# Pooled attention with a squared-ReLU feed-forward: batch 1's values pooled on GpSimd, fillers between the stages of chunk 0's softmax, split operands of chunk 0 from block 6

## The chip, the cores and the metric

The kernel runs on one core of a Trainium2 chip. The metric is device time in microseconds (us). The three timed runs of the kernel before gave 975.21, 979.04 and 979.16 us, median 979.04. The profile shows one more execution, of 978.61 us, whose span from the first to the last instruction is 976.9 us. All durations below are from that one execution.

The engines are named as in the profile: PE is TensorE's matmul, PEld its weight load, DVE is VectorE, ACT ScalarE, POOL GpSimd, SP SyncE, which issues all DMAs here.

## The reference

Attention over keys and values pooled in groups of 8, then a feed-forward with a squared ReLU:

```python
k_p = k.reshape(B, H, Sp, pool, D).mean(axis=3)      # B=8, H=8, S=576, D=64, pool=8, Sp=72
v_p = v.reshape(B, H, Sp, pool, D).mean(axis=3)
scores = scale * np.matmul(q, k_p.transpose(0, 1, 3, 2))
scores = scores - np.max(scores, axis=-1, keepdims=True)
attn = np.exp(scores)
attn = attn / (np.sum(attn, axis=-1, keepdims=True) + 1e-09)
return np.matmul(attn, v_p).astype(np.float32)
...
x = np.ascontiguousarray(attn_out.transpose(0, 2, 1, 3)).reshape(B * S, H * D)   # 4608 x 512
h = np.maximum(x @ w_in, 0.0)                         # w_in 512 x 2048, float64 in memory
return (h * h @ w_out).astype(np.float32)             # w_out 2048 x 512, float64 in memory
```

## The kernel before, in words

The 4608 tokens are worked off in 12 chunks of 384 (`CH`). For each chunk, 16 blocks of 128 hidden columns are computed: `hidden(c, fc)` makes block fc of the hidden layer of chunk c, and `project(c, fc)` adds it to the three output tiles `o_0` to `o_2`, two steps later (`LAG`). These 192 steps are the main loop. It is written out by hand: the dictionary `work` says at which step each piece of attention for later chunks, each load and each conversion of a weight is issued, and every engine takes its instructions strictly in the order of the program (`InOrder`).

Matmuls are done in two ways. In chunk 0, blocks below `SPLIT`, a product of plain float32 operands is used: `x` with `wf`, four matmuls a block, each of which the profile shows as two passes. Everywhere else both operands are split in a high and a low part (`xh`, `xl`, `w_i`) and three products are added, twelve one-pass matmuls a block. The weights arrive as float64 and become float32 in two steps: `magnitude` (two ACT instructions for each half block, called a key here) and `to_float32` (three DVE instructions for each key). `split_weights` makes the two parts (one ACT, one DVE instruction).

Before the loop stands a prologue. It pools the keys of batch 0 on DVE (`pool_k`) and those of batch 1 on POOL (`by_halves`: add the halves of the eight rows until one is left), pools the values of batch 0 by matmuls with a matrix of ones (`pool_v_pair`, tiles `vv` to `vps`), and computes the attention of chunk 0 head pair by head pair, four pairs (`NPAIR`): `transpose_q` (`qps`), `token_scores` (`sps`), the softmax on DVE and ACT (`te`, `tm`), `token_normalise` (DVE), `token_turn` (transposes `pps`, copied to `sc` by ACT), `weigh_values` (`av`, copied to `x` by ACT). The last loop of the prologue goes over the pairs p. In it stands, before the change, `pool_v_pair(1, p)` for pairs 0 and 1 of batch 1; pairs 2 and 3 are pooled at steps 2 and 3 of the main loop. For p = 2 the magnitudes of the first two keys of weights are issued on ACT, ahead of that pair's copies of `sc`.

`keep_busy(n)` issues n matmuls of the identity with itself (tile `idle`), whose result nobody reads. Before the change it is called with 16 at the start and with 2 ahead of the first scores. Its PSUM tile is from the pool `ps_h`, which the hidden blocks use too (two buffers); `ps_a` has three buffers, for everything of the attention.

All DMAs are issued by SP in one order, each after the one eight places earlier has landed. In the prologue this order is: keys, queries and values of batch 0, keys of batch 1, the first four keys of weights, the values of batch 1 (four DMAs of two heads each), then more weights. Weights, loads and several intermediate tiles share one pool of 33 buffers (`w_tile`), so a later load can wait for the reader of an earlier tile.

Of the kernel before, what the change touches and what calls it, by code (L numbers as in the profile page):

```python
# [37 lines left out]
def pooled_attn_relu2_ffn(  # L38
# [21 lines left out]
    P = 128  # L60
# [13 lines left out]
    SCALE = 1.0 / (D ** 0.5) / POOL  # L74
    LAG, QL = 2, 4

    IDLE = (16, 2)
    STB, SCB, LD, OB = 1, 2, 4, 3


    FIRST, EAGER, AHEAD = 2, 10, 4
    PRO, RATE, MARGIN = 5, 2, 1

    SPLIT = 8


    STEADY = ((-22, -18, -14, -10), (0, 1, 3, 4, 5, 6, 7, 8))
# [95 lines left out]
    def keep_busy(n):  # L183

        for i in range(0, n):
            if i % 8 == 0:
                t = ps_h.tile([P, 512], F32, name=f"idle_{n}_{i}", tag="h")
            PE.matmul(t[:, :P], lhsT=ident, rhs=ident, start=True, stop=True)


# [15 lines left out]
    def by_halves(dst, src):  # L206

        n = POOL * D // 2
        while n > D:
            GP.tensor_tensor(src[:, :n], src[:, :n], src[:, n:2 * n], op=ALU.add)  # L210
            n //= 2
        GP.tensor_tensor(dst, src[:, :D], src[:, D:2 * D], op=ALU.add)

    def pool_k(b, i):
        if i % KT == 0:
            loaded["kp", b, i // KT] = sb.tile([QT, KT, 2, D], F32, name=f"kp_{b}_{i}", tag="kp", bufs=2)
        kp, kt = loaded["kp", b, i // KT][:, i % KT], loaded.pop(("k", b, i))
        if b == 1:
            by_halves(kp[:, 0, :], kt)
            GP.tensor_tensor(kp[:, 1, :], kt[:, :D], kt[:, D:2 * D], op=ALU.add)  # L220
        else:
            DVE.tensor_reduce(kp[:, 0, :], kt.rearrange("p (o d) -> p d o", d=D), axis=AX.X, op=ALU.add)
            DVE.tensor_copy(kp[:, 1, :], kp[:, 0, :])
# [31 lines left out]
        split(kh[:, o], kl[:, o], kf[b][:, hf, :KR])  # L255

    def pool_v(b, h):
        DVE.tensor_reduce(kv[b][2][:, h, :], loaded.pop(("v", b, h)).rearrange("p (o d) -> p d o", d=D), axis=AX.X, op=ALU.add)

# [6 lines left out]
    def load_v_pair(b, p):  # L268
        vt = loaded["v", b, p] = w_tile(F32, f"vv_{b}_{p}").rearrange("s a n -> s (a n)")[:QT, :2 * EK * D].rearrange(
            "s (h j d) -> s h j d", h=2, j=EK)  # L270
        load(vt.rearrange("s h j d -> s h (j d)"), v[b, 2 * p:2 * p + 2].rearrange("h (s j) d -> s h (j d)", j=EK))

    def pool_v_pair(b, p):
        new_batch(b)
        vt = loaded.pop(("v", b, p))
        pt = ps_a.tile([P, 512], F32, name=f"vps_{b}_{p}", tag="a")
        for j in range(EK):
            PE.matmul(pt[:SP_, :2 * D], lhsT=ones[:, j, :], rhs=vt[:, :, j, :], start=j == 0, stop=j == EK - 1)

        def then():  # L280
            ACT.copy(kv[b][2][:, 2 * p:2 * p + 2, :].rearrange("s h d -> s (h d)"), pt[:SP_, :2 * D])

        return then
# [120 lines left out]
    def token_scores(c, p):  # L404
        st = live.pop((c, p))
        ss = token_banks(c, p, "sps", "o")
        segs = segments(c)
        for t in range(NQ):
            h, b = 2 * p + t // 2, segs[t % 2 % len(segs)][0]
            for j in range(2):  # L410
                two = slice(j * D, (j + 1) * D)
                PE.matmul(ss[j][:QT, t * SP_:(t + 1) * SP_], lhsT=st[two, t * QT:(t + 1) * QT],
                          rhs=kf[b][two, h // KH, h % KH * SP_:(h % KH + 1) * SP_], start=True, stop=True)
        views = [x[:QT, :NQ * SP_].rearrange("p (t n) -> p t n", t=NQ) for x in ss]

        def then():
            m = sb.tile([QT, 4, 2, NQ], F32, name=f"tm_{c}_{p}", tag="tm", bufs=2)
            e = w_tile(F32, f"te_{c}_{p}")[:QT, :, :NQ * SP_].rearrange("p i (t n) -> p i t n", t=NQ)
            e = [e[:, i] for i in range(2)]
            for i in range(2):  # L420
                DVE.tensor_reduce(m[:, 0, i], views[i], axis=AX.X, op=ALU.max)
                if c:
                    DVE.tensor_scalar(m[:, 1, i], m[:, 0, i], -SCALE, None, op0=ALU.mult)
                else:
                    DVE.tensor_tensor(e[i], views[i], m[:, 0, i].unsqueeze(2).to_broadcast([QT, NQ, SP_]), op=ALU.subtract)
            for i in range(2):
                if c == 0:
                    ACT.activation(e[i], e[i], AF.Exp, scale=SCALE)
                for t in range(NQ if c else 0):
                    ACT.activation(e[i][:, t], views[i][:, t], AF.Exp, bias=m[:, 1, i, t:t + 1], scale=SCALE)  # L430
            live[c, p] = (e, m)

        return then
# [34 lines left out]
    def weigh_values(c, p):  # L468

        if p == 0 and c == 0:  # L470
            x0.extend(w_tile(F32, f"x_{c}_{i}")[:, :, :CH] for i in range(2))
        elif p == 0:
            xts[c] = (sb.tile([P, NPAIR, CH], F32R, name=f"xh_{c}", tag="xh", bufs=2),
                      sb.tile([P, NPAIR, CH], F32R, name=f"xl_{c}", tag="xl", bufs=2))
        sc, rb = live.pop((c, p))
        av = ps_a.tile([P, 512], F32, name=f"av_{c}_{p}", tag="a")
        for b, o, n in segments(c):
            for i in range(2):
                PE.matmul(av[i * D:(i + 1) * D, o:o + n], lhsT=kv[b][2][:, 2 * p + i, :], rhs=sc[:, i, o:o + n],
                                 start=True, stop=True)  # L480

        def then():
            if c == 0:
                ACT.copy(x0[p // 2][:, p % 2, :], av[:, :CH])
                return
            xh, xl = xts[c]
            if c == 1:
                split(xh[:, p, :], xl[:, p, :], av[:, :CH])
                return
            DVE.tensor_tensor(rb, av[:, :CH], rb, op=ALU.mult)  # L490
            split(xh[:, p, :], xl[:, p, :], rb)

        return then
# [66 lines left out]
    def at(step, f, *a):  # L560
        work.setdefault(max(step, -PRO), []).append((f, a))
# [20 lines left out]
    first_keys = keys[:FIRST]  # L582
    for key in keys[:FIRST + 2]:
        land(key)
    for p in range(NPAIR):
        load_v_pair(1, p)
    for key in keys[FIRST + 2:EAGER]:
        land(key)
    issue_loads()
# [18 lines left out]
        f()  # L608
    for i in range(NKT):
        pool_k(1, i)  # L610
    for p in range(NPAIR):
        token_normalise(0, p)
        after = [token_scores(0, p + 2), pool_v_pair(1, p)] if p + 2 < NPAIR else []
        if p:
            weigh_values(0, p - 1)()
        if p == 2:
            for key in first_keys:
                magnitude(key)
        token_turn(0, p)()
        for f in after:  # L620
            f()
    to_float32(*first_keys)
    weigh_values(0, NPAIR - 1)()
    for hf in range(2):
        at(0, transpose_k, 1, hf)
        at(9 + hf, split_k, 1, hf)
    for p in range(2, NPAIR):
        at(p, pool_v_pair, 1, p)
    at(3, split_x0)


# [42 lines left out]


    last = (to_float32, split_weights)
    on_pe = (transpose_k, transpose_q, scores, token_scores, token_turn, weigh_values, pool_v_pair)
    for s in range(-PRO, len(steps) + LAG):
        todo = work.get(s, [])
        activate = hidden(*steps[s]) if 0 <= s < len(steps) else None  # L680
# [49 lines left out]
```

## Time and profile before

| what | value |
|---|---|
| median of three timed runs | 979.04 us |
| the profiled execution, its own time | 978.61 us |
| its span | 976.9 us |
| PE busy | 957.1 us (98%) |
| DVE, ACT, POOL busy | 611.6, 451.9, 332.9 us |
| start of the first hidden block (`h`) | 51.23 us |
| mean granted TensorE clock over the span | 0.983 |

A busy share says only that instructions were under way. The views used below are the page (sums over the whole span, and the span in 40 slices), the chain of waits (followed back from the last instruction, so that each piece is what the next one waited for), the timeline of one engine (start, duration, engine, line, operation, out<-in, shapes, count, and in brackets the idle time ahead and what ended it), and the table of windows (busy time of each engine in a stretch, with the granted clock as a share of full speed). All compute instructions have line 34, that of the helper which keeps them in order, so they are told apart by their tiles.

### The profile page before, as it was taken

The page shows a single profiled execution, that of the slowest core. Times are in us where ns is not written, and L with a number is a line of the kernel's source. Part 1 is how long each engine was busy: PE and PEld are TensorE (multiplying, and loading weights), DVE is VectorE, ACT ScalarE, POOL GpSimd, SP SyncE. Part 2 cuts the span into 40 slices and gives each one's busy share as a digit, 9 for nine tenths or more (in the row PEclk, how much of TensorE's full clock was granted, in tenths as well). Part 3 has the DMA queues.
Part 4 walks back from the last instruction along what each step waited for, and adds up shares of the span by engine and source line. Part 5 has one row for each costly group of instructions (what it writes and reads, how often), then busy time and mean ns, then how long its engine had stood idle before and what let it go on. Part 6 is the DMA issues. An engine that isn't in the chain of part 4 may idle for free.

```text
span 976.9 us, 13532 instructions
## 1 busy us (share of the span) xinstructions
PE 957.1 (98%) x4980; PEld 811.7 (83%) x4980; DVE 611.6 (63%) x1028; ACT 451.9 (46%) x913; POOL 332.9 (34%) x191
## 2 busy tenths in 40 slices
PE   7799999999999999999999999999999999999998
PEld 6555667888888888888888888888888888888997
DVE  7477887667765655767775656666776555453221
ACT  2487876665344344444434444443543434432322
POOL 4100044354353453434345344433434434440000
PEclk9589999999999999999999999999999999999999
DMA  9944201112112112112212101211311210100000
GB/s 275 347 143 128 80 17 65 48 52 84 48 45 74 30 33 82 33 51 79 60 43 70 44 18 55 65 40 46 100 52 29 77 31 18 58 10 9 32 1 33
DMA packets 51810, 63.64 MB, mean 65 GB/s; under 512 B 13904, under 2 KB 32928, under 8 KB 51744
## 3 DMA queue, kind: packets, MB, share of 16 engines
q1 hardware_dynamic: 51744, 62.78, 20.8%
q8 instruction: 39, 0.64, 0.3%
q14 instruction: 27, 0.22, 0.1%
HBM read 53.08 MB, written 9.68 MB: 64 GB/s over the span
## 4 chain that ended last, share of the span: by engine, by line
PE 92%; DVE 2%; DMA 2%; ACT 2%; issue 1%; SPq 1%; ACTq 0%
PE o L34 41%; PE h L34 40%; PE av L34 4%; PE sps L34 3%; PE qps L34 1%; DMA vv<-in_v_dram 1%; PE vps L34 1%; DMA k<-in_k_dram 1%; DVE wf_o L34 1%; DVE wf_i L34 1%; DMA q<-in_q_dram 1%; PE pps L34 1%; SPq L34 1%; ACT raw_i L34 0%; DVE tm L34 0%
## 5 line engine op out<-in xcount | busy, mean ns | idle before, releaser
L34 PE MATMUL h<-xh,w_i 128*128 128x384 f32 x1472 | 411.8, 340 | 0.0
L34 PE MATMUL o<-w_o,gh 128*128 128x512 f32 x1056 | 334.8, 398 | 0.0
L34 PEld LDWEIGHTS h<-xh,w_i 128*128 128x128 f32 x1472 | 269.8, 188 | 10.1 <-issue 1.0
L34 POOL PARTITION_ALL_REDUCE tot<-sc x80 | 201.4, 2564 | 209.9 <-issue 199.5
L34 PE MATMUL h<-xl,w_i 128*128 128x384 f32 x736 | 247.2, 336 | 0.0
L34 PEld LDWEIGHTS o<-w_o,gh 128*128 128x128 f32 x1056 | 192.5, 189 | 51.9 <-issue 16.5
L34 POOL PARTITION_ALL_REDUCE mx<-sc x80 | 118.4, 1527 | 319.0 <-ACT sc L34 319.0
L34 DVE TENSOR_TENSOR gl<-r,gh 128x384 fp32r<-128x384 f32 x176 | 143.6, 816 | 109.0 <-ACT gh L34 108.7
L34 PE MATMUL o<-w_o,gl 128*128 128x512 f32 x528 | 209.1, 396 | 0.0
L34 DVE TENSOR_TENSOR r<-r 128x384 f32<-128x384 f32 x160 | 105.7, 660 | 109.0 <-ACT r L34 108.6
L34 ACT CAST gh<-r 128x384 fp32r<-128x384 f32 x176 | 90.4, 514 | 149.9 <-DVE r L34 149.4
L34 PEld LDWEIGHTS h<-xl,w_i 128*128 128x128 f32 x736 | 138.2, 188 | 10.1 <-issue 2.6
L34 ACT ACTIVATE r<-h 128x384 f32<-128x384 f32 x192 | 94.0, 489 | 100.8 <-PE h L34 99.4
L34 PEld LDWEIGHTS o<-w_o,gl 128*128 128x128 f32 x528 | 99.1, 188 | 22.2
L34 DVE TENSOR_TENSOR st<-qps,st 64x384 fp32r<-64x384 f32 x80 | 60.8, 760 | 58.2 <-ACT st L34 57.4
L34 ACT CAST st<-qps 64x384 fp32r<-64x384 f32 x80 | 59.5, 743 | 56.2 <-PE qps L34 55.7
L34 ACT CAST xh<-rb 128x384 fp32r<-128x384 f32 x40 | 20.5, 513 | 94.7 <-DVE rb L34 94.7
L34 ACT ACTIVATE sc<-sc 72x384 f32<-72x384 f32 x80 | 39.7, 525 | 46.4 <-DVE sc L34 46.4
L34 DVE TENSOR_REDUCE vp<-v 72x64 f32<-72x512 f32 x48 | 50.9, 1060 | 0.0
L34 PE MATMUL av<-sc,vp 72*64 72x384 f32 (+1 forms) x256 | 46.4, 448 | 4.0 <-ACT sc L34 2.7
L34 PE MATMUL o<-wf_o,r 128*128 128x512 f32 x96 | 44.4, 598 | 0.0
L34 DVE TENSOR_REDUCE kp<-k 96x64 f32<-96x512 f32 x42 | 43.8, 1044 | 0.3 <-DMA k<-in_k_dram 0.3
(80 smaller groups left out, 707.1 us busy)
## 6 DMA issues: line engine op xcount, KB each, us to landing
k<-in_k_dram SPq DMA_DIRECT2D x48, 192.0 KB
out_dram<-ob SPq DMA_DIRECT2D x36, 256.0 KB
raw_i<-in_moe_w_in_dram SPq DMA_DIRECT2D x16, 512.0 KB
raw_o<-in_moe_w_out_dram SPq DMA_DIRECT2D x16, 512.0 KB
rb<-rd SPq DMA_DIRECT2D x80, 96.0 KB
v<-in_v_dram SPq DMA_DIRECT2D x48, 144.0 KB
q<-in_q_dram SPq DMA_DIRECT2D x30, 192.0 KB
q<-in_q_dram SPq DMA_DIRECT2D x32, 96.0 KB
```

The lines of the kernel that those rows point to most:

```text
L34: return lambda *a, **k: self.tc.keep_in_program_order(f(*a, **k))
```

## The change

Three parts. First, batch 1's values are no longer pooled by matmuls: eight loads of one head each take the place of four of two heads, and POOL adds them up by halves, right behind batch 1's keys. Second, `keep_busy` starts with 10 matmuls where 16 were, takes its PSUM tile from `ps_a`, and is called with 2 in each of the four passes of the last prologue loop. Third, chunk 0 uses split operands from block 6 on, where it was block 8.

```diff
-    IDLE = (16, 2)
+    IDLE = (10, 2)
...
-    SPLIT = 8
+    SPLIT = 6
...
-                t = ps_h.tile([P, 512], F32, name=f"idle_{n}_{i}", tag="h")
+                t = ps_a.tile([P, 512], F32, name=f"idle_{n}_{i}", tag="a")
...
     def pool_v(b, h):
-        DVE.tensor_reduce(kv[b][2][:, h, :], loaded.pop(("v", b, h)).rearrange("p (o d) -> p d o", d=D), axis=AX.X, op=ALU.add)
+        vp, vt = kv[b][2][:, h, :], loaded.pop(("v", b, h))
+        if b == 1:
+            by_halves(vp, vt)
+        else:
+            DVE.tensor_reduce(vp, vt.rearrange("p (o d) -> p d o", d=D), axis=AX.X, op=ALU.add)
...
-    for p in range(NPAIR):
-        load_v_pair(1, p)
+    for h in range(H):
+        load_v(1, h)
...
     for i in range(NKT):
         pool_k(1, i)
+    new_batch(1)
+    for h in range(H):
+        pool_v(1, h)
     for p in range(NPAIR):
         token_normalise(0, p)
-        after = [token_scores(0, p + 2), pool_v_pair(1, p)] if p + 2 < NPAIR else []
+        after = [token_scores(0, p + 2)] if p + 2 < NPAIR else []
         if p:
             weigh_values(0, p - 1)()
+        keep_busy(IDLE[1])
         if p == 2:
...
-    for p in range(2, NPAIR):
-        at(p, pool_v_pair, 1, p)
```

What PE finds between the scores of pair 2 and the first hidden block, before the change (rows of its program: operation, out<-in, shape of the output, count; the numbers at the end of a name are buffer numbers):

```order
L34 MATMUL vps_0_342<-vv_0_110,ones 72x128 x6
L34 MATMUL pps_0_0_349<-ident,te_0_226 72x96 x4
L34 MATMUL pps_0_1_350<-ident,te_0_226 72x96 x4
```

```order
L34 MATMUL vps_1_387<-vv_1_111,ones 72x128 x6
L34 MATMUL av_0_396<-sc_0_359,vp_186 64x384 x2
L34 MATMUL pps_1_0_400<-ident,te_1_259 72x96 x4
L34 MATMUL pps_1_1_401<-ident,te_1_259 72x96 x4
L34 MATMUL av_1_428<-sc_1_410,vp_186 64x384 x2
L34 MATMUL pps_2_0_437<-ident,te_2_363 72x96 x4
L34 MATMUL pps_2_1_438<-ident,te_2_363 72x96 x4
L34 MATMUL av_2_456<-sc_2_447,vp_186 64x384 x2
```

Between the two pieces stand the scores of pair 3, unchanged. The same stretch of PE's program after the change:

```order
L34 MATMUL idle_0_364<-ident 128x128 x2
L34 MATMUL pps_0_0_367<-ident,te_0_224 72x96 x4
L34 MATMUL pps_0_1_368<-ident,te_0_224 72x96 x4
```

```order
L34 MATMUL av_0_406<-sc_0_377,vp_184 64x384 x2
L34 MATMUL idle_0_410<-ident 128x128 x2
L34 MATMUL pps_1_0_413<-ident,te_1_257 72x96 x4
L34 MATMUL pps_1_1_414<-ident,te_1_257 72x96 x4
L34 MATMUL av_1_440<-sc_1_423,vp_184 64x384 x2
L34 MATMUL idle_0_444<-ident 128x128 x2
L34 MATMUL pps_2_0_452<-ident,te_2_381 72x96 x4
L34 MATMUL pps_2_1_453<-ident,te_2_381 72x96 x4
L34 MATMUL av_2_471<-sc_2_462,vp_184 64x384 x2
```

The two groups `vps` of batch 1 are gone from PE's way, and a pair of `idle` matmuls stands ahead of each `pps`.

The second place is POOL's program behind the last key of batch 1. Before, the reductions of the main loop follow there. After the change there are 24 additions first, three for each head; these are the first six and the first of the next pair:

```order
L34 TENSOR_TENSOR v_0_110<-v_0_110 72x256
L34 TENSOR_TENSOR v_0_110<-v_0_110 72x128
L34 TENSOR_TENSOR vp_323<-v_0_110 72x64
L34 TENSOR_TENSOR v_0_110<-v_0_110 72x256
L34 TENSOR_TENSOR v_0_110<-v_0_110 72x128
L34 TENSOR_TENSOR vp_323<-v_0_110 72x64
L34 TENSOR_TENSOR v_2_111<-v_2_111 72x256
```

The third place is ACT's program at step 3 of the main loop, ahead of the read of hidden block 3 (`r_3`), after the change:

```order
L34 ACTIVATE wf_i_0_693<-raw_i_0_561 128x512
L34 ACTIVATE raw_i_0_561<-raw_i_0_561 128x512
L34 CAST w_i_0_704<-wf_i_0_604 128x512
L34 ACTIVATE r_3_709<-h_3_658 128x384
L34 ACTIVATE r_3_709<-r_3_709 128x384
```

The row `CAST w_i_0_704` is new at this place; a second one, `CAST w_i_2_766`, stands ahead of `r_4`. Each has its subtraction on DVE. Before, both casts and both subtractions came in a later step, past the end of chunk 0.

More of the change, by code (lines that the diff above doesn't have):

```diff
@@ L676, in pooled_attn_relu2_ffn @@
     last = (to_float32, split_weights)
-    on_pe = (transpose_k, transpose_q, scores, token_scores, token_turn, weigh_values, pool_v_pair)
+    on_pe = (transpose_k, transpose_q, scores, token_scores, token_turn, weigh_values)
     for s in range(-PRO, len(steps) + LAG):
```

## The prediction

> **What bounds the kernel now.** First the page: the chain of waits by engine, and the clock by slices.
>
> ```profile
> PE 92%; DVE 2%; DMA 2%; ACT 2%; issue 1%; SPq 1%; ACTq 0%
> PEclk9589999999999999999999999999999999999999
> ```
>
> PE is the bound nearly everywhere, at full clock, except in the second and third slices (24 to 73 us), where the clock was halved for a while. So I read the start closely. The table of windows, cut where the clock changed (stretch, length, then busy time with count for PE, PEld, DVE, ACT, POOL, then granted clock, DMA share, GB/s):
>
> ```profile
> 1.90:5.32 3.42, 1.94 (x9) 1.94 (x10) 3.00 (x9) 0.16 (x1) 0.00 (x0) 1.00 0.89 265
> 5.32:8.73 3.41, 3.41 (x18) 3.41 (x18) 3.31 (x7) 0.00 (x0) 0.34 (x1) 1.00 1.08 270
> 15.56:18.97 3.41, 2.37 (x26) 2.06 (x23) 2.98 (x8) 1.20 (x4) 3.01 (x7) 1.00 1.09 281
> 22.38:25.80 3.42, 0.00 (x0) 0.00 (x0) 3.25 (x10) 0.00 (x0) 3.11 (x9) 1.00 1.08 310
> 25.80:29.21 3.41, 1.40 (x7) 1.43 (x8) 0.34 (x1) 0.00 (x0) 1.96 (x5) 0.50 1.09 266
> 29.21:32.62 3.41, 3.41 (x25) 3.11 (x25) 0.00 (x0) 1.33 (x3) 0.00 (x0) 0.50 1.05 355
> 32.62:36.04 3.42, 3.42 (x22) 3.01 (x20) 2.52 (x7) 0.91 (x4) 0.00 (x0) 0.50 1.04 391
> 53.10:56.52 3.42, 3.42 (x7) 1.58 (x6) 3.38 (x7) 3.42 (x7) 0.00 (x0) 0.50 0.00 0
> 56.52:59.93 3.41, 3.41 (x19) 2.19 (x17) 3.41 (x8) 3.41 (x8) 0.00 (x0) 1.00 0.52 151
> 971.28:974.69 3.41, 1.36 (x6) 0.76 (x5) 0.00 (x0) 1.76 (x3) 0.00 (x0) 1.00 0.56 216
> 974.69:976.90 2.21, 0.00 (x0) 0.00 (x0) 0.00 (x0) 0.00 (x0) 0.00 (x0) 0.50 0.06 23
> ```
>
> The clock changed at 25.80, 56.52 and 974.69 us; the distances, 30.72 and 918.17, are 9 and 269 times 3.413 us, so it is decided window by window on a fixed grid. A window without any matmul lost it (22.38 to 25.80); so did one that was 40% busy (971.28); one 69% busy kept it (15.56). A window full of 128x128 matmuls gave it back (53.10), but windows full of the smaller `vps`, `sps`, `pps` did not (29.21, 32.62). The first recorded change is 8.73; before it the column has nothing to show, and only durations tell:
>
> ```profile
> 3.38:8.73 5.35, 5.35 (x25) 5.35 (x26) 1.00 1.02 266
> 8.73:9.60 0.87, 0.87 (x9) 0.84 (x8) 1.00 1.13 270
> ```
>
> These are the `idle` matmuls alone: 0.214 us a pass up to 8.73, 0.10 behind it. Now PE's own timeline in the prologue, and what ACT does there:
>
> ```profile
> 21.23 0.90 PE L34 MATMUL sps<-kf,st 64*96 64x72 f32 x16
> 27.81 2.81 PE L34 MATMUL vps<-vv,ones 96*72 96x128 f32 x12 [5.67 <-DMA vv<-in_v_dram]
> 30.41 1.49 PE L34 MATMUL pps<-ident,te 96*72 96x96 f32 x8
> 31.29 1.52 ACT L34 COPY sc<-pps 72x384 f32<-72x384 f32 x2 [9.15 <-PE pps L34]
> 38.45 1.51 ACT L34 COPY sc<-pps 72x384 f32<-72x384 f32 x2 [0.27 <-PE pps L34]
> 25.19 0.95 DVE L34 TENSOR_TENSOR te<-te,tm 96x288 f32<-96x288 f32 x2
> 39.34 2.22 PE L34 MATMUL av<-sc,vp 72*64 72x384 f32 x4 [0.28 <-ACT sc L34]
> 41.97 0.67 ACT L34 ACTIVATE wf_i<-raw_i 128x512 f32<-128x512 f32 x1
> 44.19 1.54 ACT L34 COPY sc<-pps 72x384 f32<-72x384 f32 x2
> 51.34 0.48 ACT L34 COPY x<-av 128x384 f32<-128x384 f32 x1 [1.63 <-PE av L34]
> 60.60 0.46 ACT L34 ACTIVATE r<-h 128x384 f32<-128x384 f32 x1
> 61.12 1.24 PE L34 MATMUL h<-x,wf_i 128*128 128x384 f32 x3 [0.17 <-ACT r L34]
> 71.59 0.82 PE L34 MATMUL pps<-ident,te 96*72 96x96 f32 x8
> 43.02 3.40 SPq L34 DMA_DIRECT2D raw_o<-in_moe_w_out_dram  x2
> ```
>
> PE stood 5.67 us for batch 1's first values, lost the clock in that wait, and everything up to 56.5 us ran at half speed. From the last copy of `x` (51.34) to the read of block 0 (60.60) ACT works without a break through seven keys' magnitudes and three copies, 9.26 us, and PE's third hidden block waits for it (61.12).
>
> **Part 1: the values leave PE.** The wait of 5.67 us and the first `vps` go, the second (2.8 us at half clock) too. What is late next is the chain `pps`, copies of `sc`, `av`, next `pps`. I walk it from the end of the scores, 22.13, less 0.4 (below). At full clock a pair of `idle` takes 0.45 (four passes of about 0.11), half a `pps` 0.5 until ACT may start (the eight take 0.82 at 71.59), the copies 1.52. At half clock ACT starts 0.9 behind `pps` (31.29 after 30.41), and `av` ends 1.6 behind its copies (39.34 + 2.22 against 38.45 + 1.51); at full clock I take 0.8.
>
> Pair 0: scores to 21.7, idle to 22.2, copies 22.7 to 24.2, `av` to 25.0, idle to 25.5. Pair 1's normalised `te` ends at 26.14 less 0.4, about then; its copies run from 26.0 to 27.5, `av` to 28.3. For pair 2 ACT first copies `x` and does the two first keys, 0.4 + 2.2 us (41.97 to 44.19), so its copies of `sc` run from 31.0 to 32.5. In the 3.4 us behind 28.7 PE has one `pps` and the start of an `av`, about 1.2 us or 35%. By the 40% row I take it that the clock falls here, near 32.5. Then `av` runs to 34.1, idle (0.85 now) to 35.0, the copies of pair 3 from 35.9 to 37.4, `av` to 39.0. The last copy of `x` then starts at 39.0 where it was 51.34: **12.3 us** earlier. ACT's 9.26 us follow unchanged, whatever PE does beside them; the first hidden block at half clock lies beside them as it did. With the clock kept all through, the same walk ends its copies at 32.5, `av` at 33.3, idle at 33.8, copies at 35.8, `av` at 36.6: 14.7 us.
>
> In the loop the other two groups go:
>
> ```profile
> 63.97 1.31 PE vps L34 x12
> 70.44 1.31 PE vps L34 x12
> 87.48 2.58 PE h L34 x8
> 131.09 2.09 PE h L34 x12
> ```
>
> They are on the chain, between blocks that PE works off back to back: **2.6 us**. What must follow faster is ACT and DVE, with these waits between 61 and 128 us:
>
> ```profile
> ACT vp L34 <- PE vps L34: 1.7, 1, 1.7
> DVE xl L34 <- ACT xh L34: 7.2, 3, 3.8
> DVE tm L34 <- PE sps L34: 1.9, 1, 1.9
> ```
>
> ACT gets 1.7 us from the very wait that goes, DVE has 3.8 in one piece: enough.
>
> POOL's additions cost by the rows of the keys:
>
> ```profile
> L34 POOL TENSOR_TENSOR k<-k 96x256 f32<-96x256 f32 x6 | 4.8, 792 | 6.0 <-DMA k<-in_k_dram 6.0
> L34 POOL TENSOR_TENSOR kp<-k 96x64 f32<-96x64 f32 x12 | 4.1, 358 | 0.5
> L34 POOL TENSOR_TENSOR k<-k 96x128 f32<-96x128 f32 x6 | 2.7, 450 | 0.5
> 36.40 0.82 DVE L34 TENSOR_TENSOR te<-te,tm 96x288 f32<-96x288 f32 x2
> ```
>
> One head is 0.79 + 0.45 + 0.36, eight heads 12.8 us, from 28 to 41 or so. The first reader is chunk 1's `av` in step 4, well behind the third hidden block, and POOL has nothing else until then (0.00 in the windows from 29.21 on): free. DVE slows a little beside POOL: the same operation took 0.95 us with POOL busy (25.19) and 0.82 without (36.40). Pair 2's `pps` may come 1.3 us late, since ACT is at the keys until 31.0, so I cost this at nothing, between 0 and 1 us. The eight loads carry the bytes of the four, the DMA engines are full either way (share above 1.0), and the weights wait behind the same bytes. One later load now waits for POOL's last addition, to 41 or 43 us, with all of SP's queue behind it; but that queue stood at 43.02 for its buffers before, and ACT takes the keys in it behind block 0.
>
> **Part 2: fillers.** Four times two `idle` are in the walk. Six fewer at the start let PE's first transposes begin at 3.38 + 20 x 0.214 = 7.65, not 9.60. The gain is between 0 and 1.95 us; DVE's pooling of the keys and the landing of batch 0's values are unmoved behind them, so I take 0.4.
>
> **Part 3: split operands.** Blocks 6 and 7 become 12 passes of 2.09 us, from 8 of 2.58: 1.0 us. Two casts and two subtractions move ahead of them, on a DVE that has at least 1.9 us of room at that place (its wait for `sps`). Between 0 and 1.0 us of gain, or 0.5 of loss if DVE becomes late; I take **0.5**.
>
> **Sum.** 12.3 + 2.6 + 0.5 = 15.4 us off the profiled execution's 978.61: **963.2 us**. That execution lies 0.4 below the median, 979.04; I leave this out.
>
> **The rivals.** *The clock holds to the end.* 14.7 + 2.6 + 0.5: 960.8 us. For it: the longest gap in the walk is under 2 us. The Trainium skill, "TensorE: Matmul & The Clock Gate", in "Why this matters for your kernels", asks only for no idle gap above some 3 us; by that rule this rival would be the forecast. Against it stands the window at 971.28, whose matmuls ended 2.05 us before the clock went.
>
> *The fillers don't do their work, and PE is never warm.* 20 cold passes are 4.27 us. One full window on the grid lies inside that only if an edge falls in the right 0.86 of 3.41 us; a window 57% busy (1.90) did not lift the clock, a full one did. If a share between is needed and is missed, the small matmuls cannot lift it later (29.21, 32.62). Then the four `vps` of batch 0 take 1.4 us more each (2.8 against 1.3 to 1.4) and the three `sps` some 0.7: the scores of pair 2 end at 22.13 + 5.6 + 2.1 = 29.8 less the 0.4 or so, and the first `pps` starts near 30.1 (30.41 before). A stage lasts 0.9 + 1.52 + 1.6 + 0.85 = 4.9, pair 2 has the keys' 2.6 ahead of its copies: `av` of pair 1 ends at 39.0, the copies at 43.1, `av` at 44.7, idle at 45.6, copies at 48.0, `av` at 49.6. The last copy of `x` starts 1.7 us earlier than before. With 3.1: 973.8 us. I hold it for the less likely case, since transposes and two more `idle` follow the burst with hardly a gap. The Trainium skill, "TensorE: Matmul & The Clock Gate", in "What's actually happening", says that at least one busy window of about 3.4 us lifts the clock and that the windows run free of the kernel's start; taken strictly, this 973.8 us would come in three executions of four, and the trace of one execution can't exclude it.
>
> *Slower: the clock is lost into the loop.* If PE, waiting for ACT behind block 1, leaves each window under the share that lifts the clock, steps 0 to 7, some 36 us of dense work from 61.12 on, run at half speed: 36 - 15 = 21 us more, 1000 us. It decides from the point where windows of `h` and `o` stay under some 60%. Against: a slowed PE fills its windows by itself, and 53.10 lifted at once.
>
> **How the numbers follow.** Forecast (clock up at the start, lost once late) 0.45; held throughout 0.25; never up 0.23; slower 0.04; the rest something unseen. The two first are 2.4 us apart; with 2 us for the bounds of parts 2 and 3 they fill 958.5 to 967. To leave out no more than 0.2 the range must reach the cold case: 958.5 to 975. A measurement can tell about 0.5%, 4.9 us, from no change, so faster means under 974.1. That holds for both first cases and about half of the cold one: 0.82; same 0.13; slower 0.05.
>
> **What would show it.** No wait of PE for `vv`; the first `h` near 39, the third near 49; granted clock 1.0 from about 9 us, perhaps 0.5 between 32 and 45; eight passes of `h` fewer ahead of step 6. Wrong would be: passes of 0.2 us behind the first burst (cold), ACT's stretch behind the last copy of `x` longer than 9.3 us, or PE waiting for `w_i` or `r` in steps 3 to 8.

## The result, and the profile after

| | before | after |
|---|---|---|
| median of the timed runs | 978.86 us (975.21 to 979.16) | 963.93 us (963.50 to 964.38) |
| ratio | | 0.9856, 95% interval 0.9832 to 0.988 |
| the profiled execution, its own time | 978.61 us | 964.33 us |
| its span | 976.9 us | 962.6 us |
| end of the last matmul | 972.64 us | 959.14 us |
| start of hidden blocks 0, 2, 3, 4, 10 | 51.23, 61.12, 67.69, 75.18, 110.42 | 39.83, 49.73, 56.20, 62.48, 96.77 |

The change takes 14.9 us off by the medians and 14.25 by the spans of the two profiled executions; 15.4 was forecast. (One execution of one experiment below, the first combination, took 3295 us, with every matmul some 2.7 times as long; its trace is left out, and no ratio counts it.)

The page of the kernel after: the chain by engine, and the granted clock by slices.

```profile
PE 88%; DVE 5%; DMA 4%; ACT 2%; issue 1%; SPq 0%; ACTq 0%; DVEq 0%
PEclk9799999999999999999999999999999999999999
```

Only the second slice (24 to 48 us) is still low, and DVE now has 5% of the chain, where it had 2. The windows, on this execution's grid (its first change of clock is at 8.99):

```profile
22.65:26.06 3.41, 3.41 (x34) 2.23 (x32) 3.27 (x9) 2.61 (x5) 3.10 (x8) 1.00 0.98 360
26.06:29.47 3.41, 2.81 (x16) 1.36 (x15) 3.21 (x8) 2.43 (x5) 2.77 (x6) 1.00 0.80 216
29.47:32.89 3.42, 1.54 (x12) 0.90 (x11) 3.25 (x10) 3.42 (x7) 3.13 (x6) 1.00 1.01 292
39.71:43.13 3.42, 3.42 (x6) 1.85 (x6) 2.00 (x3) 3.20 (x7) 3.11 (x7) 0.50 1.05 387
43.13:46.54 3.41, 3.41 (x19) 2.33 (x18) 3.41 (x5) 3.41 (x9) 3.18 (x5) 1.00 1.07 300
```

The clock goes at 32.89, behind a window in which PE was busy 1.54 of 3.42 us, and comes back at 43.13, behind a window full of `h`: 10.24 us cold, where it was 30.72. PE's own timeline, from the scores of pair 2 to the fourth hidden block, and ACT's last copy of `x` and first read of a block:

```profile
21.13 0.90 PE L34 MATMUL sps<-kf,st 64*96 64x72 f32 x16
21.96 0.71 PE L34 MATMUL idle<-ident 128*128 128x128 f32 x4
22.51 0.83 PE L34 MATMUL pps<-ident,te 96*72 96x96 f32 x8
27.54 1.57 PE L34 MATMUL av<-sc,vp 72*64 72x384 f32 x4 [0.60 <-ACT sc L34]
32.65 2.24 PE L34 MATMUL av<-sc,vp 72*64 72x384 f32 x4 [1.11 <-ACT sc L34]
34.82 1.23 PE L34 MATMUL idle<-ident 128*128 128x128 f32 x4
35.83 1.49 PE L34 MATMUL pps<-ident,te 96*72 96x96 f32 x8
39.83 4.47 PE L34 MATMUL h<-x,wf_i 128*128 128x384 f32 x8
49.73 2.85 PE L34 MATMUL h<-x,wf_i 128*128 128x384 f32 x8 [1.17 <-ACT r L34]
56.20 2.85 PE L34 MATMUL h<-x,wf_i 128*128 128x384 f32 x8 [1.04 <-ACT r L34]
39.93 0.48 ACT L34 COPY x<-av 128x384 f32<-128x384 f32 x1 [1.63 <-PE av L34]
49.18 0.51 ACT L34 ACTIVATE r<-h 128x384 f32<-128x384 f32 x1
```

The wait of 5.67 us for `vv` is gone. ACT's stretch behind the last copy of `x` is 49.18 - 39.93 = 9.25 us, the 9.26 of before. PE's wait for `r` ahead of block 2 grew from 0.17 to 1.17 us, and the one ahead of block 3 (1.04) is new. Where the time came from, by the lead over the kernel before at the same block: 11.4 us at block 0, 11.4 at block 2, 11.5 at block 3, 12.7 at block 4, 13.65 at block 10, 13.5 at the last matmul, and 0.75 more behind it. So the prologue gave 11.4, the two groups that left the loop 1.3 together, the split operands 0.8 (0.95 up to block 10; PE's wait for `te` in step 10 then grew from 1.29 to 1.56). The 0.75 is not a matter of the last stores: SP issues the last of them 0.65 us behind the last matmul and has waited for it by 2.7 us behind it, both before and after. It lies in the closing of the program, and it goes with the first part of the change: from the last matmul to the end of the span it is 3.47 to 3.49 us in all nine traces kept here with the values on POOL, 4.22 to 4.24 in all four with them on PE. Why stays open.

### The profile page after: what moved, and what is told of

Same layout as the page of the kernel before. It is cut to its first block, busy times and chain, and to the rows that moved or that the text cites. A ratio compares the mean times of both kernels' runs of the same rounds, so it can differ in the third digit from the quotient of the medians.

```text
span 962.6 us, 13481 instructions
## 1 busy us (share of the span) xinstructions
PE 946.1 (98%) x4944; PEld 803.6 (83%) x4944; DVE 615.0 (64%) x1028; ACT 451.5 (47%) x909; POOL 348.8 (36%) x215
## 4 chain that ended last, share of the span: by engine, by line
PE 88%; DVE 5%; DMA 4%; ACT 2%; issue 1%; SPq 0%; ACTq 0%; DVEq 0%
PE o L34 41%; PE h L34 39%; PE av L34 3%; PE sps L34 3%; DVE wf_o L34 2%; DVE wf_i L34 1%; PE qps L34 1%; DMA raw_o<-in_moe_w_out_dram 1%; DMA v<-in_v_dram 1%; DMA k<-in_k_dram 1%; ACT te L34 1%; DMA vv<-in_v_dram 1%; DMA raw_i<-in_moe_w_in_dram 1%; DVE tm L34 1%; DVE w_i L34 1%
## 5 line engine op out<-in xcount | busy, mean ns | idle before, releaser
L34 PE MATMUL h<-xh,w_i 128*128 128x384 f32 x1488 | 416.9, 341 | 0.0
L34 PEld LDWEIGHTS h<-xh,w_i 128*128 128x128 f32 x1488 | 272.8, 188 | 10.6 <-issue 1.4
L34 PE MATMUL h<-xl,w_i 128*128 128x384 f32 x744 | 249.9, 336 | 0.0
```

The source lines that it names most:

```text
L34: return lambda *a, **k: self.tc.keep_in_program_order(f(*a, **k))
```

## The experiments

In the table, the start of a hidden block and the end of the last matmul are read from each run's timeline, the loss of the clock from its windows; the time is the median of its own runs. The names are explained below.

| run | time, us | clock lost at (us), for | block 0 | block 3 | block 4 | block 10 | last matmul ends |
|---|---|---|---|---|---|---|---|
| before | 978.86 | 25.8, 30.7 us | 51.23 | 67.69 | 75.18 | 110.42 | 972.64 |
| after | 963.93 | 32.9, 10.2 us | 39.83 | 56.20 | 62.48 | 96.77 | 959.14 |
| values alone | 964.42 | 29.0, 13.7 us | 38.74 | 55.07 | 61.35 | 96.59 | 958.35 |
| fillers alone | 979.74 | 20.4, 37.6 us; 119.3, 3.4 us | 53.96 | 70.42 | 77.91 | 113.16 | 976.00 |
| split alone | 978.39 | 20.7, 34.1 us; 116.3, 3.4 us | 52.26 | 68.77 | 76.26 | 110.55 | 973.23 |
| no fillers in the loop over pairs | 963.95 | 27.6, 13.7 us; 102.7, 3.4 us | 38.85 | 55.15 | 61.43 | 95.71 | 958.69 |
| fillers behind `pps` | 964.95 | 55.0, 3.4 us; 102.8, 3.4 us | 36.82 | 54.31 | 62.28 | 96.57 | 959.30 |
| one addition a head | 963.52 | 33.7, 10.2 us; 102.0, 3.4 us | 40.12 | 55.34 | 61.52 | 95.79 | 958.56 |
| groups late, on PE | 969.38 | 26.1, 17.1 us | 39.81 | 58.21 | 65.69 | 99.96 | 961.62 |
| value loads earlier | 964.57 | 20.3, 23.9 us; 102.2, 3.4 us | 40.70 | 55.90 | 62.18 | 96.47 | 959.41 |
| both moves | 963.24 | 25.4, 6.8 us; 49.3, 3.4 us | 38.58 | 55.48 | 61.66 | 95.94 | 958.04 |
| combination | 962.80, 963.84 | 26.1, 6.8 us | 38.97 | 55.29 | 61.57 | 95.84 | 958.21 |

### The three parts, each alone

Values alone is the kernel before with the values on POOL and nothing else (the loads and `pool_v` are those of the change):

```diff
...
+    new_batch(1)
+    for h in range(H):
+        pool_v(1, h)
...
-        after = [token_scores(0, p + 2), pool_v_pair(1, p)] if p + 2 < NPAIR else []
+        after = [token_scores(0, p + 2)] if p + 2 < NPAIR else []
...
-    for p in range(2, NPAIR):
-        at(p, pool_v_pair, 1, p)
```

> Part 1 alone (values of batch 1 on POOL; 16 matmuls at the start, no fillers in the loop, split operands from block 8). Theory A (the gain comes from the wait for batch 1's values, which is gone, and from the six matmuls a group that left PE): nearly all of the gain is here, last copy of x near 40 (51.34 before, 39.93 after), the first h near 40, time 964 to 966 us. Rival B (without fillers the share of PE in the windows behind the scores falls under the limit and the clock goes one or two windows earlier than 32.9): granted clock 0.5 already from about 26 or 29 us, last copy of x at 41.5 to 43, time 966.5 to 969.

Measured: 964.42 us, ratio to before 0.9844 (0.983 to 0.9859). The whole gain is in this part. The clock goes at 28.99, 3.9 us earlier than after the change, as rival B had it, but without its price: the last copy of `x` starts at 38.85, 1.1 us *earlier* than in the changed kernel. Its timeline, from the same end of the scores (22.03) to the first hidden block:

```profile
21.13 0.90 PE L34 MATMUL sps<-kf,st 64*96 64x72 f32 x16
21.96 0.85 PE L34 MATMUL pps<-ident,te 96*72 96x96 f32 x8
27.43 1.58 PE L34 MATMUL av<-sc,vp 72*64 72x384 f32 x4 [0.59 <-ACT sc L34]
32.54 2.24 PE L34 MATMUL av<-sc,vp 72*64 72x384 f32 x4 [0.55 <-ACT sc L34]
34.71 1.50 PE L34 MATMUL pps<-ident,te 96*72 96x96 f32 x8
38.74 4.77 PE L34 MATMUL h<-x,wf_i 128*128 128x384 f32 x8
```

At pair 2's `av` the two timelines are 0.11 us apart (32.54, 32.65). Behind it the changed kernel has two `idle` at half clock ahead of `pps`, 1.0 us (34.82 to 35.83), on the path.

Fillers alone:

```diff
-    IDLE = (16, 2)
+    IDLE = (10, 2)
...
-                t = ps_h.tile([P, 512], F32, name=f"idle_{n}_{i}", tag="h")
+                t = ps_a.tile([P, 512], F32, name=f"idle_{n}_{i}", tag="a")
...
             weigh_values(0, p - 1)()
+        keep_busy(IDLE[1])
```

> Part 2 alone (10 matmuls at the start, two fillers in each pass, their tile from the other pool; values of batch 1 still on PE). Theory A: PE still stands for batch 1's values until 27.8 us, two fillers are 0.45 us of a stall of 5.7, so the clock is lost near 26 as before: within 1 us of before, 978 to 979.5. Rival B (the fillers carry the clock through): clock kept behind 26, time near 970, since half clock from 27.8 to 56.5 cost before some 8 us on the path.

Measured: 979.74 us, ratio 1.0005 (0.999 to 1.002). No gain, as theory A had it, though the clock went at 20.4 and not near 26.

Split alone:

```diff
-    SPLIT = 8
+    SPLIT = 6
```

> Part 3 alone (split operands from block 6). Theory A (what blocks 6 and 7 save on PE mostly stays): blocks 6 and 7 last 2.1 us each where they lasted 2.6, the lead over before at block 8 is 1.0 us, and 0.3 of it is given back to waits for te by block 11: 0.7 us less, 978. Rival B (the casts and subtractions that move ahead make DVE late): PE waits for r or te in steps 4 to 8, no gain or up to 0.5 us of loss.

Measured: 978.39 us, ratio 0.998 (0.9964 to 0.9996). From block 4 to block 10 it gains 0.95 us (76.26 to 110.55 is 34.29, before 35.24), and PE waits for no `r` or `te` there: theory A. The 0.3 us that it was to give back by block 11 are not seen (the wait for `te` in step 10 is 1.29 us, as before). In the profiled execution a window then lost the clock and took it back:

```profile
112.85:116.26 3.41, 2.12 (x28) 1.57 (x29) 2.35 (x7) 1.83 (x9) 0.00 (x0) 1.00 0.62 210
```

The kernel before has the same thin stretch at step 10 (a wait of 1.3 us for `te`), and its profiled execution kept the clock there. Where the grid lies differs from execution to execution (the first change of clock was at 8.73 before, 8.99 after, between 6.39 and 9.03 in the others), and decides which stretch shares a window with what.

### The fillers taken out

```diff
             weigh_values(0, p - 1)()
-        keep_busy(IDLE[1])
```

> The changed kernel without the two fillers in each pass of the last prologue loop. Theory A (the path there is ACT's copies and what PE does between them, the fillers only hold the clock, and one window more or less without them doesn't matter): clock lost at 29.5 or 32.9, 963.5 to 966 us. Rival B (the fillers are what holds the clock): clock lost at 26.1, last copy of x 2 us or more later than 39.93, 966 to 968. Rival C (the fillers are themselves on the path, 0.45 to 0.9 us a pass): the last copy of x comes 1 to 2 us earlier than 39.93, 962 to 963.

Measured: 963.95 us against 963.93. The window that lost the clock:

```profile
24.21:27.62 3.41, 2.07 (x13) 0.82 (x10) 3.17 (x9) 2.08 (x5) 3.10 (x8) 1.00 0.81 220
```

The fillers do hold the clock 5.3 us longer (32.89 against 27.62), and it is worth nothing: without them the last copy of `x` starts at 38.96, not 39.93, of which 0.4 is an earlier end of the scores (21.62 against 22.03). Theory A had the time; the 0.97 us are at the edge of rival C's 1 to 2. At this place the fillers cost about what the clock that they hold is worth.

### What holding the clock is worth

If it is to be held, then by matmuls where PE waits for ACT anyway, behind `pps`:

```diff
+    AHEAD_OF, BEHIND = (0, 0, 4, 0), (0, 3, 9, 3)
...
             weigh_values(0, p - 1)()
-        keep_busy(IDLE[1])
+        keep_busy(AHEAD_OF[p])
...
-        token_turn(0, p)()
+        turned = token_turn(0, p)
+        keep_busy(BEHIND[p])
+        turned()
```

> The changed kernel with the fillers of the last prologue loop moved: none ahead of the transposes pps but four ahead of pair 2's, and 3, 9 and 3 behind the pps of pairs 1, 2 and 3, where PE waits for ACT's copies anyway. Theory A (with PE busy in those waits the clock holds to the main loop, and av and pps of pairs 2 and 3 at full clock shorten the path): clock 1.0 throughout, last copy of x at 36.3 to 37, where the run without fillers had 38.96; ACT's 9.3 us behind it follow unless the weights land too late; 961 to 962.5 us. Rival B (the path there is ACT's alone and the clock is worth nothing): last copy of x within 0.5 us of 38.96 although the clock holds, 963.5 to 964.5. Rival C (the prologue gains but the gain is lost in the loop, where DVE is late): last copy of x at 36.5, hidden block 12 no earlier than in the run without fillers, 963.5.

Measured: 964.95 us, no gain. The clock held through the prologue, and the last copy of `x` started at 36.92, 2.0 us earlier than without fillers and 3.0 earlier than in the changed kernel; the prediction's two walks had 2.4 us between them. By block 4 all of it was gone (62.28 against 61.43 and 62.48). Blocks 0, 2 and 3 in PE's timeline:

```profile
36.82 2.85 PE L34 MATMUL h<-x,wf_i 128*128 128x384 f32 x8
46.75 2.85 PE L34 MATMUL h<-x,wf_i 128*128 128x384 f32 x8 [1.73 <-ACT r L34]
54.31 4.54 PE L34 MATMUL h<-x,wf_i 128*128 128x384 f32 x8 [2.13 <-ACT r L34]
```

and the window in which the second wait lies:

```profile
51.56:54.97 3.41, 1.28 (x4) 0.49 (x3) 3.31 (x10) 3.38 (x8) 0.00 (x0) 1.00 1.04 341
```

PE now waits 1.73 and 2.13 us for `r`, and that wait, in which PE is busy for 1.28 of 3.41 us, costs the clock, so that block 3 lasts 4.54 us. Behind the prologue ACT and DVE set the pace: rival C. What made DVE late is the next section.

### The additions on POOL beside DVE

What made `r` of block 1 late? Here six of the eight rows of batch 1's values are left out of the sums, so that POOL has one addition a head instead of three; the fillers are those of the changed kernel:

```diff
         if b == 1:
-            by_halves(vp, vt)
+            GP.tensor_tensor(vp, vt[:, :D], vt[:, D:2 * D], op=ALU.add)
```

> The changed kernel with one addition on POOL for each head of batch 1's values, where it has three: the sums of six of the eight rows are left out, so batch 1's attention is not the reference's. Theory A (POOL's additions beside DVE's weight conversion at 41 to 51 us slow DVE, which made r of block 1 late and cost the first of the two vps groups that left the loop): the conversions take 0.68 us each throughout, PE's wait for r ahead of the hidden block 3 falls from 1.04 to under 0.3 us, and that block starts 0.8 to 1.4 us earlier than at 56.20; 962.5 to 963.2 us if it is kept. Rival B (ACT's own chain sets r of blocks 0 and 1): block 3 within 0.3 us of 56.20, 964 us. Rival C (the loads of weights that stood behind POOL in SP's queue are the cause): DVE's conversions unchanged in length but started earlier.

Measured: 963.52 us. DVE's timeline while it converts keys 3 to 7 of the weights, first of the changed kernel:

```profile
41.01 0.65 DVE L34 TENSOR_SCALAR wf_o<-wf_o 128x512 f32<-128x512 f32 x1 [3.98 <-ACT wf_o L34]
42.47 1.10 DVE L34 SCALAR_TENSOR_TENSOR wf_o<-raw_o,wf_o 128x512 uint32<-128x512 uint32 x1
44.56 2.09 DVE L34 SCALAR_TENSOR_TENSOR wf_i<-wf_i,raw_i 128x512 uint32<-128x512 uint32 x2
50.99 0.44 DVE L34 TENSOR_REDUCE tm<-sps 96x4 f32<-96x288 f32 x1
```

and with one addition:

```profile
41.31 0.43 DVE L34 TENSOR_SCALAR wf_o<-wf_o 128x512 f32<-128x512 f32 x1 [5.47 <-ACT wf_o L34]
42.59 0.69 DVE L34 SCALAR_TENSOR_TENSOR wf_o<-raw_o,wf_o 128x512 uint32<-128x512 uint32 x1
43.90 1.29 DVE L34 SCALAR_TENSOR_TENSOR wf_i<-wf_i,raw_i 128x512 uint32<-128x512 uint32 x2
49.39 0.45 DVE L34 TENSOR_REDUCE tm<-sps 96x4 f32<-96x288 f32 x1
```

The same five keys take 8.1 us where they took 10.0. `tm`, which stands behind them, comes at 49.39, not 50.99; ACT's exponentials and then its read of block 1 follow it, and PE's wait ahead of block 3 (1.04) is gone:

```profile
50.09 2.85 PE L34 MATMUL h<-x,wf_i 128*128 128x384 f32 x8 [0.97 <-ACT r L34]
55.34 2.74 PE L34 MATMUL h<-x,wf_i 128*128 128x384 f32 x8
61.52 2.74 PE L34 MATMUL h<-x,wf_i 128*128 128x384 f32 x8
```

From block 2 to block 4 the kernel before takes 14.06 us, the changed one 12.75, this one 11.43: 1.31 us less a group, so without the contention the two groups are worth the 2.6 us of the forecast. Theory A, at that place. In the time little of it is seen, since the profiled execution lost a window at step 10 (block 10 is 0.98 us ahead of the changed kernel's, the last matmul 0.58). The loads that waited behind POOL (rival C) are not it: the conversions started no earlier.

The run with fillers behind `pps` lost its lead at the same place. Its five keys began 3 us sooner and met more of the additions, which ran to 46.83 there:

```profile
38.00 0.64 DVE L34 TENSOR_SCALAR wf_o<-wf_o 128x512 f32<-128x512 f32 x1 [1.84 <-ACT wf_o L34]
49.10 0.44 DVE L34 TENSOR_REDUCE tm<-sps 96x4 f32<-96x288 f32 x1
```

That is 11.1 us for them, 10.0 in the changed kernel, 8.1 with one addition. A clock held through the prologue with one addition a head was not run, so what the held clock is worth without this contention stays open.

### The wait or the work?

```diff
-        after = [token_scores(0, p + 2), pool_v_pair(1, p)] if p + 2 < NPAIR else []
+        after = [token_scores(0, p + 2)] if p + 2 < NPAIR else []
...
-    for p in range(2, NPAIR):
+    for p in range(NPAIR):
         at(p, pool_v_pair, 1, p)
```

Against the kernel before; 10 matmuls at the start and split operands from block 6 besides.

> Batch 1's values stay on PE, but all four groups in steps 0 to 3 of the main loop and none in the prologue; no fillers in the loop over pairs, 10 matmuls at the start, split operands from block 6. Theory A (the prologue's gain is the wait that left PE's queue, whoever does the pooling; POOL is only worth the PE time of the groups in the loop, less the waits for r in which a group can hide): last copy of x within 0.7 us of the run without fillers (38.96), then 4 x 1.31 us of PE work of which 1.5 to 2.5 hide in the waits ahead of the hidden blocks 2 and 3: 966.5 to 968.5 us. Rival B (the pooling itself, on POOL, is what pays): above 970 us. Rival C (POOL's contention costs as much as PE's work): 964 to 965.5.

Measured: 969.38 us (967.46 to 971.51), ratio 0.99 (0.9878 to 0.9923). The last copy of `x` starts at 39.91, as in the changed kernel (0.95 behind the run without fillers, 0.25 more than expected, at a clock lost 1.6 us sooner), so taking the wait out of PE's queue is enough for the prologue, whoever adds. The four groups then cost 3.3 us up to block 4, against the run without fillers (25.88 against 22.58 us from block 0). Theory A holds for the profiled execution (967.6); the median is 0.9 above its range. With the two small parts in it, 10 of the 15 us come without POOL.

### The loads earlier, both moves, and all together

Value loads earlier (no fillers in the loop over pairs):

```diff
-    for key in keys[:FIRST + 2]:
+    for key in keys[:FIRST]:
         land(key)
     for h in range(H):
         load_v(1, h)
-    for key in keys[FIRST + 2:EAGER]:
+    for key in keys[FIRST:EAGER]:
```

> The changed kernel without the fillers in the loop over pairs, and with the loads of batch 1's values ahead of the third and fourth key of weights in SP's queue. Theory A (POOL's additions slow what DVE does beside them, so it matters when they run): they run 3 to 4 us earlier and end near 42 instead of 46, the conversions behind 43 us take 0.68 us again, hidden block 3 starts 0.4 to 1 us earlier than at 55.15 in the run without fillers; against it DVE's normalising of pairs 1 and 2 is slower by some 0.3 us. 963 us, between 962.5 and 964. Rival B (no such contention, or it is off the path): block 3 unchanged within 0.3 us, 964.

Measured: 964.57 us; a miss, and badly aimed. POOL's first value addition started at 27.50, where it was 27.71 without the move: POOL is at batch 1's keys until then, the landing was not what it waited for. The execution also lost the clock early, with PE busy for 55% of a window (16.84 to 20.25), so the prologue ended 1.85 us later and the additions met fewer conversions. From block 0 to block 3 it took 15.20 us, the run without fillers 16.30: contention by another accident.

Both moves is this with the fillers behind `pps`.

> The same combination without the fillers in the waits: batch 1's value loads ahead of the third key, fillers behind pps. Theory A (the single windows are worth 1 to 2 us): clock lost for one window or more at about 20, 50 or 102 us, by where the grid lies; 961.5 to 963 us, 1 to 2 us more than the combination with them. Rival B (the windows are beside ACT's and DVE's work and cost nothing): within 0.5 us of it.

The combination has fillers at five places more, those of the main loop in columns of a hidden block's PSUM bank that the block doesn't use:

```diff
+    WAITS, BEFORE_AV = {1: 4, 2: 2}, {10: 5}
...
+    def fill(t, n):
+        for i in range(n):
+            PE.matmul(t[:, CH:CH + P], lhsT=ident, rhs=ident, start=True, stop=True)
...
+    fill(ps_h.tile([P, 512], F32, name="warm_0", tag="h"), 4)
+    after.append(pool_v_pair(0, 3))
+    transpose_q(0, 2)()
+    fill(ps_h.tile([P, 512], F32, name="warm_1", tag="h"), 2)
...
+            if f is weigh_values and s in BEFORE_AV:
+                fill(banks[steps[s]], BEFORE_AV[s])
...
+        if s in WAITS:
+            fill(banks[steps[s]], WAITS[s])
```

> A combination: the changed kernel with batch 1's value loads ahead of the third key of weights, the fillers of the pairs' loop placed behind pps (4 ahead of pair 2's; 3, 9 and 3 behind those of pairs 1 to 3), and fillers in the waits that remain: 4 behind batch 0's third group of values and 2 ahead of the last qps (19 to 21 us), 4 and 2 behind blocks 1 and 2, 5 ahead of the av of step 10. Theory A (three things were left: the clock lost in the prologue, some 3 us; POOL beside DVE's conversions, some 1.3 us; single windows lost in waits, 0.6 to 1.7 us each, by where the grid lies): clock 1.0 from the first lift to the end, last copy of x at 36.5 to 37.5, PE's wait for r ahead of block 3 under 0.8 us, 960 to 961.5 us, 2.5 to 4 us less than the changed kernel. Rival B (ACT and DVE behind the prologue set the pace, and what is won ahead of them is waited away, as in the run with fillers behind pps): clock held, but block 12 within 0.7 us of the changed kernel's, 963 to 964.5.

> The changed kernel once more, on the same chip as the two combinations: 964 us, between 963.4 and 965.

> The combination of all three (value loads of batch 1 earlier, fillers behind pps, fillers in the waits) a second time, for a trace of it. Theory A (the clock is held): clock 1.0 from the first lift to the end, last copy of x at 36.5 to 37.5, 962 to 963.5 us as in its first runs. Rival B (behind the prologue ACT and DVE set the pace, so that holding the clock there is worth nothing): the hidden block 3 at 55 us or later although the first block starts at 37, and PE waiting for r ahead of blocks 2 and 3 for 3 us or more together.

Measured: both moves 963.24 us, the combination 962.80 and 963.84 in its two turns, the changed kernel beside the first of them 965.38 (963.75 to 967.53). Against before the ratios are 0.9843 (0.9824 to 0.9863), 0.9834 (0.9813 to 0.9855), 0.9842 (0.9826 to 0.9858) and 0.9865 (0.9843 to 0.9886): they overlap, and that the combination beats the changed kernel is not shown. (The 965.38 is itself a miss, above its 963.4 to 965.) In three executions of the combination the mean granted clock was 1.000, and they took 962.3 to 962.8 us; two of the changed kernel beside them, at 0.994, took 963.75 and 964.05. By these, a prologue and a loop without any loss of clock are worth at most 1 to 1.8 us, since the loads move too, and not the 2.5 to 4 of theory A. The medians of that turn lie 2.6 us apart, but the other four executions of the changed kernel had a lower clock (0.984 to 0.993). The first median lies between the ranges of theory A and rival B, the second in rival B's; the one trace, which lost the clock, has the conditions of neither. The trace of its second turn, first the window in which it lost the clock, then PE's timeline:

```profile
22.68:26.09 3.41, 2.62 (x25) 1.52 (x23) 3.20 (x9) 2.42 (x5) 3.10 (x8) 1.00 0.80 211
```

```profile
25.67 1.57 PE L34 MATMUL pps<-ident,te 96*72 96x96 f32 x8 [0.71 <-DVE te L34]
35.17 0.87 PE L34 MATMUL av<-sc,vp 72*64 72x384 f32 x4
38.97 2.85 PE L34 MATMUL h<-x,wf_i 128*128 128x384 f32 x8
48.93 2.85 PE L34 MATMUL h<-x,wf_i 128*128 128x384 f32 x8 [0.68 <-ACT r L34]
55.29 2.85 PE L34 MATMUL h<-x,wf_i 128*128 128x384 f32 x8 [0.49 <-ACT r L34]
```

Here the clock was lost at 26.09 in spite of 77% busy, and the fillers that then ran at half clock ahead of pair 2 put the `av` to 35.17, 2.5 us later than without any (32.69). Block 3 starts at 55.29, 0.9 us ahead of the changed kernel's, as block 0 does.

## Why the prediction was right, point by point

The forecast was 963.2 us, with the clock up at the start and lost once near 32.5; 963.93 was measured (964.33 in the profiled execution), and the clock went at 32.89. The terms:

| term | forecast | measured |
|---|---|---|
| prologue (last copy of `x`) | 12.3 | 11.4 (51.34 to 39.93) |
| two groups less in the loop | 2.6 | 1.3 |
| split operands | 0.5 | 0.8 |
| behind the last matmul | 0 | 0.75 |
| sum | 15.4 | 14.25 |

That the sum comes so close is in part luck: the first two terms fell 2.2 us short, and 0.75 of that came back behind the last matmul, for which the prediction had no term.

**The values.** Right in mechanism: values alone has the whole gain, and the groups moved to the loop on PE give back, in the profiled execution, about what they cost there (967.56 us against 963.92 without fillers; 3.3 of it up to block 4). ACT's 9.26 us behind the last copy of `x` were the next thing, to 0.01 us.

**The walk through the pairs.** The place of the clock's fall was right, behind the window that the walk had nearly empty: the table had 1.2 us of work, 35%, in the window behind 28.7; the trace has 1.54 us, 45%. The walk came out 0.9 short, and was 0.8 short already at pair 2's copies (31.77 against 31.0). Of the front gain of 0.4, 0.3 did not come (scores end at 22.03, not 21.7; 16 matmuls at the start gave the same 22.03, 10 in other executions 21.6 to 22.9, the latest of them where the clock went near 20). The rest are tenths at full clock, taken too short in pairs 0 and 1: a pair of `idle` ahead of `pps` takes 0.55 (21.96 to 22.51), not 0.45, and ACT starts its copies 0.65 behind `pps` (26.65 after 26.00), not 0.5. The steps at half clock behind it held to 0.1.

**Fillers.** The prediction put them into the walk as a given and left open that they are a cost. They were: values alone reached the last copy of `x` 1.1 us earlier without them, at a clock that fell sooner. The rival in which the clock holds throughout needs other fillers; made so, it gave its 2.4 us in the prologue (2.0 measured) and lost them behind it, which the prediction didn't follow: it took ACT's stretch as the last thing late, and not DVE's and POOL's.

**The loop groups.** The step that was mis-sized. "I cost this at nothing, between 0 and 1 us" was said of POOL's additions beside DVE, with the normalising of pair 2 in view, and an end at 41. They ran to 46.84, and met the conversion of the weights at 41 to 51, behind which `tm`, `te` and `r` of block 1 stand. One addition a head showed it: 1.3 us, a little over the bound. One of the prediction's own signs of being wrong came with it, PE waiting for `r` in steps 3 to 8: 1.04 us ahead of block 3. The profile before had shown DVE without a gap at that point of the program (3.41 of 3.41 us in the window at 56.52).

**POOL's own sum** was off for the same reason. The groups of instructions of the changed kernel, between 27 and 48 us (line, operation, shapes, count, then busy time and mean ns of one, then idle time before):

```profile
L34 POOL TENSOR_TENSOR v<-v 72x256 f32<-72x256 f32 x8 | 9.6, 1195 | 0.5 <-DMA v<-in_v_dram 0.5
L34 POOL TENSOR_TENSOR v<-v 72x128 f32<-72x128 f32 x8 | 4.4, 549 | 0.6
L34 POOL TENSOR_TENSOR vp<-v 72x64 f32<-72x64 f32 x8 | 3.2, 396 | 0.6
```

17.2 us, where 12.8 were summed from 792, 450 and 358 ns.

**Split operands** gave 0.95 us alone and in the change up to block 10; DVE was not late. The value taken, 0.5, was the middle of the bounds.

**Rivals.** Never warm: not seen. All profiled executions with 10 matmuls at the start were lifted there, some by a window that was not full (88% and 94% busy, in the runs with one addition and with the value loads earlier). Slower: a window behind block 1 or 2 did lose the clock in two experiments whose prologue was faster, but one window of `h` and `o` lifted it again: 1.7 us (4.54 against 2.85), not 21.

## What to carry to other kernels

A wait in the queue of an in-order engine costs the wait, what it does to the clock, and all that stands behind it: moving it off is worth more than the work that moves with it. A filler belongs where the engine waits anyway; ahead of work that is on the path it costs its own length, twice that at half clock, and a clock held ahead of a stretch where another engine sets the pace buys little. When work goes to POOL, the cover to check is not POOL's idle time but what DVE does on the path in those very microseconds.

## What the runs showed of the hardware

**The clock's window.** First a window of the run with fillers behind `pps`, behind which the clock stayed, then one of the run with both moves, behind which it went:

```profile
44.73:48.15 3.42, 1.69 (x13) 1.01 (x10) 3.42 (x6) 2.49 (x5) 1.94 (x3) 1.00 0.46 135
21.99:25.40 3.41, 2.68 (x27) 1.68 (x24) 3.24 (x10) 2.59 (x5) 3.10 (x7) 1.00 0.81 191
```

All changes of clock lie whole multiples of 3.413 us apart, and the grid's place differs by execution. Its rule is no plain share of busy time. Windows 45, 54, 55 and 61% busy lost the clock, and so did four of 72 to 79%, in which `pps` and `av` ran, with or without `sps` (22.64 with the groups late on PE, 25.58 with values alone, 22.68 in the combination, and the second one here). Many of 66 to 70% kept it, and so did the first one here, 49% busy, and one of 53% (6.39 with one addition a head). The Trainium skill, "TensorE: Matmul & The Clock Gate", "Why this matters for your kernels", asks for no idle gap above some 3 us; the window of 77% holds no gap over 0.71 us (the wait of `pps` at 25.67), so these runs disagree. The Trainium skill, in "Part 4: PE-mode transpose" of the same page, says that transposes don't count as busy in the same way. `pps`, `qps` and `kps` are transposes, but leaving them out doesn't sort the windows either: some 65% would be left of the window of 77%, and some 45% of one of 66% that kept the clock (17.43 to 20.84 with fillers behind `pps`). What weighs a window stays open.

**POOL against DVE.** They slow each other. While DVE converted the first two keys (33.5 to 37.0 in the changed kernel), two of POOL's additions took 3.85 us together, 1.25 just behind:

```profile
34.31 3.85 POOL L34 TENSOR_TENSOR v<-v 72x256 f32<-72x256 f32 x2
38.51 1.25 POOL L34 TENSOR_TENSOR v<-v 72x256 f32<-72x256 f32 x2
```

and a DVE conversion 1.10 instead of 0.69. The Trainium skill, "SBUF — State Buffer", "SBUF: two separate sides", describes it: a DVE instruction with two SBUF inputs, or in a two-port mode, and a GpSimd one exclude each other for the whole instruction. The traces agree as far as they go: the 0.41 us that the conversion lost is of the length of one of POOL's additions, 0.32 to 0.72 us where nothing held them up, and the first of the two additions in 3.85 us lasted 3.32, past the end of all four conversions with two inputs that DVE ran from 34.55 to 37.03.
